# A transposed tile's copy handed from VectorE to ScalarE, three small moves in the same kernel

## The chip, the cores and the metric

One Trainium2 chip, one of its cores. The metric is the device time of one execution in microseconds (us), the median of the timed runs: 208.69 us for the kernel before (three runs, 208.44 to 209.05). The profile is of one execution; its span, from the first to the last instruction, is 206.6 us, so about 2 us of the timed figure lie outside the span.

## What is computed

A block-sparse attention, whose output goes straight into a two-matrix feed-forward stage.

```python
# q, k, v: (4, 8, 768, 64); block 32, window 16
k_sum = k.reshape(B, H, nb, 32, D).max(axis=3)          # 24 block keys
v_sum = v.reshape(B, H, nb, 32, D).mean(axis=3)         # 24 block values
scores_l = scale * q @ k.T, kept where |i - j| < 16
scores_s = scale * q @ k_sum.T + log(32)
a = softmax([scores_l, scores_s])
x = (a @ [v, v_sum])  ->  (B*S = 3072 tokens, H*D = 512)
h = x @ w_in                                             # 512 x 2048
g = h / (1 + exp(-1.702 h))                              # quick gelu
out = g @ w_out                                          # 2048 x 512, fp32
```

## The kernel before

The 3072 tokens are eight half-batches of 384, called units here: u = 0 and 1 belong to batch 0, u = 2 and 3 to batch 1, and so on. For each unit the kernel makes attention scores (ps_s), exponentials (a_sb, on ScalarE), values (ps_av), normalised rows (x, on VectorE), transposes these on TensorE into ps_x, and copies ps_x to SBUF as xT, one copy for each half (g = 0 and 1) of the 512 features. Then `ff_in` (L660) multiplies xT by w_in into PSUM tiles ph, ScalarE takes gelu of each into gT, and `ff_out` (L809) multiplies gT by w_out into po.

Every engine's work stands in program order: the wrapper `_Ordered` (L18) records each instruction so, and nothing overtakes on one engine. So the order in which Python calls are made is the schedule, and it is written out by hand:

- **The head** (L933 to L1028) loads batch 0's keys and queries in fp32 from two issuing engines, SyncE and ScalarE, pair of heads by pair (`load_k`, `load_q`, L83 and L93), then casts (kb, qb), transposes (ps_k, ps_q), copies (kx, qT), takes block maxima (`k_max`, L422, into ksz) and computes unit 0's attention. `exp_soon` (L929) runs a one-element exponential on a tile called gate, so that ScalarE loads the exponential's function table there and not ahead of the first real exponential.
- **Between units 0 and 1** (L1109 to L1122) the output stage of unit 0 has twelve slots. In each, `ff_out` runs four matmuls; then `beside` (L1059) runs what the table `plan0` (L1054) gives for the slot: q's transposes, scores s0 to s3, values v0 and v1, and the transposes with their copies, x0 and x1 (`tx`, L647). After some slots `w_sums` (L825) forms four sums of a quarter of w_out into the tiles ta and tb, on VectorE. Later stages use them for Strassen-Winograd products. After slot 11 `ff_in` of unit 1 starts; its first three ph tiles need x0 for the first six matmuls and x1 for the next six.
- **Unit 1's input stage** also transposes batch 1's keys (ps_t), duplicates batch 1's value rows on VectorE (`v_odd`, L143) and sums them by blocks on TensorE (`vsum`, L316, into ps_vs). The value rows come by six loads of GpSimd's queue (`load_vc`, L137). After these, `halo_dmas` (L347) and `sum_dmas` (L360) bring the edge rows and block sums to their places in vw.
- **The last input stage** (`ff_in_pairs`, L702) handles units 6 and 7 together with seven products, M1 to M7, in place of eight. M6(0) accumulates onto M1(0)'s PSUM tile, and VectorE adds m (M7(0), which ScalarE copied out) to it; M5(0) accumulates onto the same PSUM tile once VectorE has read it. `plain()` (L773) is an ordinary product of four matmuls into a tile of its own.

DMA issues are tied by semaphores: the built program gives the issues of SyncE and ScalarE eight semaphores in turn, and those of GpSimd another eight. A DMA that gets a semaphore for a second time is issued only when the earlier DMA on it has landed. In the head, the fifth issue of ScalarE (keys of pair 3) and its sixth (queries of pair 3) wait in this way; so do GpSimd's issues nearly everywhere.

PSUM tiles of 2 KB (tag mm: po, ph, ps_x, ps_q) rotate through four buffers, those of 4 KB (tag big: ps_s, ps_t, ps_vs, ps_av of unit 1) through two.

Of the kernel before, what the change touches and what calls it, by code (L numbers as in the profile page):

```python
# [35 lines left out]
def kernel(  # L36
# [16 lines left out]
    NP = H // 2  # L53
# [11 lines left out]
    dve = _Ordered(tc, nc.vector)  # L65
    act = _Ordered(tc, nc.scalar)
# [16 lines left out]
    def load_k(p):  # L83
        if p == 0:
            early["k"] = stage.tile([128, NP, 2, 2, JH, D], F32, name="kf", tag="kf")
        t = early["k"][:, p]
        for i in range(2):
            (act if i else sp).dma_start(out=t[:, i].rearrange("p h r d -> p h (r d)"),
                         in_=k[0, 2 * p:2 * p + 2, i * HALF:(i + 1) * HALF]
                         .rearrange("h (p r) d -> p h (r d)", r=JH))  # L90
        raw["k", p] = t
# [159 lines left out]
    def clear0(eng):  # L251

        for p in range(NP):
            clear_kx(eng, p, 0)
        clear_vw(eng, 0)
        eng.memset(ksz, 0.0)
        eng.memset(vs4, 0.0)
        v6 = vs4.rearrange("p (a g) c -> p a g c", g=4)
        for g in range(4):
            eng.memset(v6[g * 32:g * 32 + nb, :, g, D:D + 1], float(block))  # L260
# [386 lines left out]
    def tx(g, m, eng=dve):  # L647
        ps = pmm.tile([128, 2, HALF], F16, name="ps_x", tag="mm")
        for i in range(2):
            for j in range(JH):  # L650
                pe.transpose(out=ps[:, i, j * 128:(j + 1) * 128],
                             in_=x2[g][:, i, j].rearrange("p h d -> p (h d)"), identity=identx)
        copy(eng, xTT[m][g], ps)
# [48 lines left out]
    def ff_in_pairs(u, early):  # L702

        (b11, b21), (b12, b22) = xTT
        xs = castp2.tile([128, 4, 2, HALF], F16, name="xsum", tag="kb")
        t = [xs[:, m] for m in range(4)]
        big = [psb.tile([128, 1024], F32, name="pw_in", tag="big") for _ in range(2)]
        mm = [pmm.tile([128, 512], F32, name="px_in", tag="mm") for _ in range(4)]
        X, V = ([m[:, 0:HALF] for m in mm[n:n + 2]] for n in (0, 2))
        Y = [big[0][:, n:n + HALF] for n in (0, 512)]  # L710
        L = big[1][:, 0:HALF]

        def gelu(w, f, src):
            act.activation(out=gT[w % 2][:, f, :], in_=src, func=ACT.Gelu_apprx_sigmoid)

        def one(w, f, ps):
            for ko in range(KO):
                pe.matmul(out=ps, lhsT=w_in_sb[:, ko, f * 128:(f + 1) * 128], rhs=xT[w % 2][ko],
                          start=(ko == 0), stop=(ko == KO - 1))
            gelu(w, f, ps)  # L720

        def prod(ps, a, b, i, first=False):
            for k in range(2):
                pe.matmul(out=ps, lhsT=a[:, k, i], rhs=b[:, k], start=(first and k == 0),
                          stop=(k == 1), skip_group_check=True)

        ws = [wt["s"][:, n] for n in range(4)]
        hold = {}

        def f0(i):  # L730
            return 2 * (NI - WI + i)

        def M1(i):
            x = X[i % 2]
            prod(x, wt[0, 0], b11, i, True)
            dve.tensor_copy(out=Y[i % 2], in_=x)

        def M7(i):
            v = V[i % 2]
            prod(v, ws[2], t[2], i, True)  # L740
            hold[i] = attp.tile([128, HALF], F32, name="m7", tag="x2")
            copy(act, hold[i], v)

        def M6(i):
            x = X[i % 2]
            prod(x, ws[1], t[1], i)
            dve.tensor_add(V[i % 2], x, hold[i])

        def M2(i):
            y = Y[i % 2]  # L750
            prod(y, wt[0, 1], b21, i)
            gelu(u, f0(i), y)

        def M5(i):
            x = X[i % 2]
            prod(x, ws[0], t[0], i)
            hold[i, 2] = attp.tile([128, HALF], F32, name="c22", tag="a_sb")
            dve.tensor_add(hold[i, 2], x, hold[i])

        def M4(i):  # L760
            v = V[i % 2]
            prod(v, wt[1, 1], t[3], i)
            gelu(u, f0(i) + 1, v)
            gelu(u + 1, f0(i) + 1, hold[i, 2])

        def M3(i):
            x = X[i % 2]
            prod(x, ws[3], b22, i)
            gelu(u + 1, f0(i), x)

        n, rest = 2 * (NI - WI), list(range(2 * (NI - WI)))

        def plain():  # L773
            one(u + 1, rest.pop(0), L)

        for f, ps in zip(range(n), (Y[0], X[1], V[1], L, Y[1], X[1])):
            if f == 2:
                M1(0)
            one(u, f, ps)
        dve.tensor_sub(t[2], b22, b12)  # L780
        dve.tensor_add(t[1], t[2], b11)
        dve.tensor_sub(t[0], b12, b11)
        dve.tensor_sub(t[3], b21, t[1])
        M2(0)
        M7(0)
        plain()
        M6(0)
        for i in range(1, WI):
            M1(i)
            for f in (M7, M5) if i == 1 else (M5, M7):  # L790
                f(i if f is M7 else i - 1)
            M4(i - 1)
            M6(i)
            M3(i - 1)
            M2(i)
            plain()
            if i == 2:
                early(0, NI - WI)
        i = WI - 1
        M5(i)  # L800
        M4(i)
        early(NI - WI, NI)
        plain()
        M3(i)
        assert not rest
# [123 lines left out]
    def exp_soon():  # L929
        act.activation(out=gate[:, 1:2], in_=gate[:, 0:1], func=ACT.Exp)  # L930


    dve.memset(gate, 0.0)  # L933
    for p in range(NP):
        load_k(p)
        load_q(p, 0)
    exp_soon()
    clear0(dve)
    dve.tensor_copy(out=identx, in_=ident)
    dve.memset(vs[:, :, D:VC], float(block))  # L940
# [102 lines left out]
    for p in range(NP):  # L1043
# [8 lines left out]
             6: ["v0", "s2", "s3"], 8: ["x0"], 9: ["v1", "S0", "S1"], 11: ["x1", "S2", "S3"]}  # L1052

    plan0 = {-1: ["q0", "q1"], 0: ["q2"], 1: ["q3"], 2: ["s0", "s1"], 4: ["s2", "s3"],  # L1054
             7: ["v0", "v1"], 9: ["x0"], 11: ["x1"]}

    w51 = vw[1].rearrange("p (j e) h c -> p j e h c", e=2)

    def beside(u, slot):  # L1059
        b, half = u // 2, u % 2  # L1060
        for what in (plan0 if u == 1 else plan1).get(slot, ()):
            i = int(what[1])
            if what[0] == "t":
                tq1(i, dve if i % 2 else act)
            elif what[0] == "q":
                q_turn(i, 1)
                q_copy(i, dve, 1)
            elif what[0] == "s":
                scores(b, half, i)
                if half and i == NP - 1:  # L1070
                    gelu_soon()
            elif what[0] == "S":
                scores(b, 1, i)
                if i == NP - 1:
                    gelu_soon()
            elif what[0] == "v":
                values(b, half, i, u == 1)
            else:
                tx(i, half)

    for u in range(2):
        todo = {}
        if u == 0:
            for p in range(NP):
                todo.setdefault(12 + p // 2, []).append(lambda p=p: cast_q(dve, p, 1))
        else:
            def value_rows():
                vsum(1, range(NJ))
                block_sums()
                halo_dmas(w51, 0)  # L1090
                sum_dmas(w51, 0)
                load_kc(2, range(6, H))
                load_vc(2)
                load_qc(2)

            todo = {0: [lambda: tk(0, 1)], 3: [lambda: tk(1, 1)], 5: [lambda: v_odd(1)],
                    9: [value_rows], 10: [lambda: tk(2, 1)], 13: [lambda: tk(3, 1)]}
            ff_in(u, range(3))
        for nt in range(0 if u else N0, NT):
            if u == 0 or nt > 2:  # L1100
                ff_in(u, (nt,))
            for f in todo.get(nt, ()):
                f()
        exp_soon()
        if u == 0:
            beside(1, -1)
            load_qc(1)
            load_kc(2, range(6))
        order = [(ms, part) for ms in range(JH) for part in range(4)]  # L1109
        if u == 0:  # L1110

            order = [(ms, part) for part in range(4) for ms in range(JH)]
        for i, (ms, part) in enumerate(order):
            ff_out(u, ms, part)
            beside(u + 1, i)
            if u == 0 and i in (4, 7, 10):
                w_sums(i // 3 - 1)
            if u == 1 and i == 2:
                w_sums(3)
            if u == 1 and i == 3:  # L1120
                for g in range(2):
                    xk(g, 2)  # L1122
# [22 lines left out]
    for b in range(1, B):  # L1145
# [3 lines left out]
        u = 2 * b  # L1149
# [95 lines left out]
```

The softmax here doesn't subtract the row's maximum and nothing guards it: scores larger than these inputs give would overflow.

## Time and profile before

| | before |
|---|---|
| time, median of 3 | 208.69 us |
| span of the profiled execution | 206.6 us |
| TensorE busy | 199.2 us, 96% of the span |
| VectorE busy | 145.1 us, 70% |
| ScalarE busy | 123.5 us, 60% |
| GpSimd busy | 91.5 us, 44% |
| chain that ended last | TensorE 90%, VectorE 7%, ScalarE 1%, issue 1% |
| ScalarE copy ps_x to xT, 128x768, mean of 2 | 806 ns |
| VectorE copy ps_x to xT, 128x768, mean of 4 | 553 ns |
| ScalarE function table load, mean of 10 | 1283 ns |
| the four instructions of one `w_sums`, means | 416, 425, 417, 417 ns |

How to read it: nearly the whole chain is TensorE, so a change can bring time only where TensorE's own chain has a hole, and can cost time wherever it opens one. The chain's VectorE part lies mainly in the head and between units 0 and 1. A row of the timeline has the start, the duration (from the first start to the last end, where several are merged), the engine, the operation with its tiles, the count, and, in brackets, how long the engine had been idle and what released it. Matmul durations overlap, so a row's end can lie some 0.15 us past the next row's start.

### The profile page before, as it was taken

To read this page: it belongs to the slowest core of one execution; us is meant where nothing else is said; L and a number is where in the kernel's file an instruction comes from. 1 tells how busy PE (TensorE), PEld (TensorE's weight loads), DVE (VectorE), ACT (ScalarE), POOL (GpSimd) and SP (SyncE) were. 2 spreads that over 40 slices of the span, in tenths; PEclk is the share of its full clock that TensorE was granted. 3 is DMA by queue.
4 is the path that set the end of the run, shared out by engine and by line. 5 is a ranking of instruction groups with operands and counts; after the bars stand their busy time and mean duration, and the time that the engine had idled before them with its cause. 6 is when DMAs were issued, how large, how long until landed. Compare 5 with 4: busy or idle time off the path is not lost.

```text
span 206.6 us, 5570 instructions
## 1 busy us (share of the span) xinstructions
PE 199.2 (96%) x2212; PEld 136.1 (66%) x2212; DVE 145.1 (70%) x421; ACT 123.5 (60%) x235; POOL 91.5 (44%) x162
## 2 busy tenths in 40 slices
PE   7899999998999999999999999999999999999992
PEld 3667565545665666566888865567887855568882
DVE  6677845796966769936757688589885956669431
ACT  0877676634685489677743657677626477881220
POOL 5996889498899951425999100401000000000000
PEclk9999999999999999999999999999999999999999
DMA  6999999999999999999999999993054250000323
GB/s 187 296 166 207 247 246 217 174 171 222 150 155 153 156 128 120 216 133 131 114 129 202 108 274 158 139 165 59 3 129 102 53 179 0 3 2 25 105 76 102
DMA packets 95009, 28.94 MB, mean 140 GB/s; under 512 B 82880, under 2 KB 92000, under 8 KB 94984
## 3 DMA queue, kind: packets, MB, share of 16 engines
q0 software_dynamic: 67920, 14.88, 80.7%
q1 hardware_dynamic: 25432, 12.53, 30.9%
q10 hardware_dynamic: 1632, 1.18, 1.8%
q8 instruction: 17, 0.28, 0.6%
q14 instruction: 8, 0.07, 0.1%
HBM read 27.26 MB, written 6.29 MB: 162 GB/s over the span
## 4 chain that ended last, share of the span: by engine, by line
PE 90%; DVE 7%; ACT 1%; issue 1%; DVEq 0%
PE ph L28 30%; PE px L28 15%; PE pw L28 8%; PE po L28 7%; PE px_in L28 6%; PE ps_av L28 4%; PE ps_s L28 4%; PE py L28 4%; PE pw_in L28 4%; PE ps_w L28 2%; PE ps_t L28 1%; PE ps_k L28 1%; DVE ta L28 1%; PE ps_x L28 1%; DVE x L28 1%; DVE kb L28 1%
## 5 line engine op out<-in xcount | busy, mean ns | idle before, releaser
L28 PE MATMUL ph<-xT,w_in_sb 128*128 128x384 f16 x384 | 65.5, 326 | 1.2 <-DVE xT L28 1.2
L28 PEld LDWEIGHTS <-w_in_sb 128*128 128x128 f16 x462 | 44.3, 98 | 30.3 <-issue 1.7
L28 ACT ACTIVATE gT<-ph 128x384 f16<-128x384 f32 x96 | 45.6, 490 | 21.3 <-PE ph L28 21.0
L28 PEld LDWEIGHTS <-gT 128*128 128x128 f16 x384 | 36.1, 98 | 11.8
L28 ACT ACTIVATE a_sb<-ps_s 128x768 bf16<-128x768 f32 x28 | 21.1, 806 | 8.8 <-PE ps_s L28 8.8
L28 PE MATMUL po<-w_out_sb,gT 128*128 128x512 f16 x96 | 23.4, 380 | 0.0
L28 PEld LDWEIGHTS <-ss 128*128 128x128 f16 x216 | 20.7, 98 | 2.6
L28 ACT ACTIVATE t<-px 128x256 f32<-128x256 f32 x21 | 8.0, 383 | 21.9 <-PE px L28 21.9
L28 DVE TENSOR_TENSOR a_sb<-a_sb,mk 128x768 bf16<-128x768 bf16 x28 | 15.2, 555 | 7.5 <-ACT a_sb L28 6.4
L28 PE MATMUL px<-ta,ss 128*128 128x256 f16 x144 | 18.7, 273 | 0.0
L28 PE MATMUL pw<-tb,gT 128*128 128x256 f16 x144 | 18.7, 273 | 0.0
L28 ACT ACT_TABLE_LOAD x10 | 12.8, 1283 | 6.0 <-DMA kf<-in_k_dram 5.9
L28 DVE TENSOR_TENSOR x<-ps_av,rc 128x384 f16<-128x384 f32 x28 | 15.6, 557 | 1.0
L28 POOL DMA_DIRECT2D vw<-in_v_dram x18 | 15.9, 936 | 0.0
L28 POOL DMA_DIRECT2D vw<-vw x12 | 6.6, 575 | 18.9 <-DVE vw L28 17.2
L28 POOL DMA_DIRECT2D kb<-in_k_dram x16 | 13.2, 856 | 3.5 <-DMA w_out_sb<-in_moe_w_out_dram 3.1
L28 POOL DMA_DIRECT2D qb<-in_q_dram x16 | 13.4, 920 | 2.9 <-DMA vw<-in_v_dram 2.9
L28 DVE TENSOR_TENSOR osb<-pw,t 128x256 f32<-128x256 f32 x18 | 7.5, 421 | 9.0 <-PE pw L28 5.3
L28 DVE TENSOR_TENSOR ss<-gT 128x384 f16<-128x384 f16 (+4 forms) x18 | 7.5, 418 | 5.4 <-ACT gT L28 5.4
L28 PEld LDWEIGHTS <-kx 64*128 64x128 bf16 x400 | 7.2, 95 | 5.8 <-issue 4.0
L28 DVE TENSOR_REDUCE ks<-kx 128x24 bf16<-128x768 bf16 x8 | 7.6, 946 | 3.7 <-DMA kx<-kb 3.7
L28 PE MATMUL ps_s<-qT,kx 64*128 64x64 bf16 (+3 forms) x400 | 9.1, 190 | 0.9 <-DVE kb L28 0.7
(120 smaller groups left out, 311.0 us busy)
## 6 DMA issues: line engine op xcount, KB each, us to landing
out_dram<-osb SPq DMA_DIRECT2D x18, 256.0 KB, 5.0
vw<-in_v_dram POOLq DMA_DIRECT2D x18, 128.0 KB, 6.3
w_in_sb<-in_moe_w_in_dram POOLq DMA_DIRECT2D x4, 512.0 KB, 10.6
w_out_sb<-in_moe_w_out_dram POOLq DMA_DIRECT2D x4, 512.0 KB, 19.8
kb<-in_k_dram POOLq DMA_DIRECT2D x16, 96.0 KB, 5.4
qb<-in_q_dram POOLq DMA_DIRECT2D x16, 96.0 KB, 7.5
out_dram<-osb SPq DMA_DIRECT2D x12, 128.0 KB, 1.7
vw<-vs POOLq DMA_DIRECT2D x6, 148.5 KB, 4.2
```

The lines of the kernel that those rows point to most:

```text
L28: r = f(*a, **kw)
```

## The change

Four edits. (1) The copies of unit 1's x0 and x1 go to ScalarE, and x1 moves from slot 11 to slot 10 of unit 0's output stage, so that its transposes come ahead of the last four po matmuls. (2) The first `w_sums` moves from slot 4 to slot 3, ahead of the scores s2 and s3. The aim of both is that xT stands ready when unit 1's input stage begins. (3) In `ff_in_pairs` M6(0) is put before the first plain product, so that VectorE's addition runs beside that product. (4) In the head the exponential's table is loaded before the last keys and queries are issued, so that ScalarE loads it while it would wait to issue them.

```diff
@@ ff_in_pairs
         M2(0)
         M7(0)
+        M6(0)
         plain()
-        M6(0)
         for i in range(1, WI):
@@ the head
     dve.memset(gate, 0.0)
-    for p in range(NP):
+    for p in range(NP - 1):
         load_k(p)
         load_q(p, 0)
     exp_soon()
+    load_k(NP - 1)
+    load_q(NP - 1, 0)
     clear0(dve)
@@ plan0
-             7: ["v0", "v1"], 9: ["x0"], 11: ["x1"]}
+             7: ["v0", "v1"], 9: ["x0"], 10: ["x1"]}
@@ beside
-                tx(i, half)
+                tx(i, half, act if u == 1 else dve)
@@ the output stage of unit 0
-            if u == 0 and i in (4, 7, 10):
+            if u == 0 and i in (3, 7, 10):
                 w_sums(i // 3 - 1)
```

In the built program this is the whole change of order on each engine, with one thing that the lines do not say: the semaphores of the head's loads are dealt out anew. Before, the fifth issue of SyncE waits for the first keys of SyncE and its sixth for the first queries; ScalarE's fifth waits for its own first keys and its sixth for its own second keys. After, they wait in this order for ScalarE's first keys, SyncE's first keys, ScalarE's second keys, and the first queries. And of the three first ph tiles of unit 1, the third takes the PSUM buffer of x1's transposes, where before it took that of the third po tile.

## The prediction

> **What bounds the kernel now.** I read the page's shares first: TensorE busy 96% of the span, and 90% of the chain that ended last. Only a hole in TensorE's work can bring time. Then the chain in order of time, to find where it leaves TensorE. It does so in the head, between units 0 and 1, and once in the last input stage; from 47.66 us to there it is TensorE without a break. Last the timeline of these stretches. Columns of the chain: start, duration, engine and tile. The head:
>
> ```profile
> 6.40 0.34 PE ps_q L28 x3
> 6.76 0.56 DVE qT L28
> 7.32 1.03 DVE kb L28 x2
> 8.35 0.86 DVE ksz L28
> 9.22 1.04 DVE kb L28 x2
> ```
>
> ScalarE's timeline (start, duration, engine, operation, and in brackets the idle time before it and its releaser) shows there:
>
> ```profile
> 5.85 1.28 ACT L28 ACT_TABLE_LOAD   x1 [5.85 <-DMA kf<-in_k_dram]
> ...
> 7.25 0.79 ACT L28 ACTIVATE kx<-ps_k 128x768 bf16<-128x768 f32 x1
> ```
>
> The load stands behind an issue that waited for a DMA, and kx behind the load; ps_k was done at 6.15. But the chain runs through VectorE's queue, and kx is not on it. Between units 0 and 1:
>
> ```profile
> 43.66 0.41 DVE L28 TENSOR_TENSOR ta<-w_out_sb 128x512 f16<-128x512 f16 x1
> ...
> 44.79 0.41 DVE L28 TENSOR_TENSOR tb<-w_out_sb,ta 128x512 f16<-128x512 f16 x1
> 44.84 0.50 PE L28 MATMUL ps_x<-identx,x 128*128 128x128 f16 x6
> ...
> 45.13 0.55 DVE L28 COPY xT<-ps_x 128x768 f16<-128x768 f16 x1
> 45.59 0.41 DVE L28 TENSOR_TENSOR ta<-w_out_sb 128x512 f16<-128x512 f16 x1
> ...
> 45.73 1.15 PE L28 MATMUL ph<-xT,w_in_sb 128*128 128x384 f16 x6 [0.39 <-DVE xT L28]
> ...
> 47.05 0.55 DVE L28 COPY xT<-ps_x 128x768 f16<-128x768 f16 x1
> 47.66 1.14 PE L28 MATMUL ph<-xT,w_in_sb 128*128 128x384 f16 x6 [0.78 <-DVE xT L28]
> ```
>
> This is the hole to see: x0's transposes were ready at 43.28 and x1's at 45.34, but both copies stand in VectorE's queue behind four sums each. TensorE idles 0.39 and 0.78 us. The last input stage, in the chain:
>
> ```profile
> 170.24 0.34 PE px_in L28 x2
> 170.67 0.58 DVE px_in L28
> 171.29 1.62 PE px_in L28 x8
> ```
>
> M5(0) at 171.29 waits for VectorE's addition to M6(0). M6(0), M1(1) and M7(1) run from 170.24 to 171.22, so the hole is 0.07 us. Last, what could stop a TensorE that comes earlier:
>
> ```profile
> 52.19 1.68 POOL L28 DMA_DIRECT2D qb<-in_q_dram  x2 [0.85 <-DMA vw<-in_v_dram]
> ...
> 53.94 0.52 PE L28 MATMUL ps_vs<-vw,E 128*32 128x128 bf16 x24
> ...
> 60.87 1.36 POOL L28 DMA_DIRECT2D vw<-vs  x2
> ...
> 67.02 0.57 PE L28 MATMUL ps_av<-vw,a_sb 128*64 128x65 bf16 x24
> ```
>
> GpSimd still waits at 52.19 for value loads that ps_vs needs. In the trace's landing records the last of the six lands at 52.66 and the second vw<-vs, which ps_av needs, at 65.69. TensorE passes 1.28 and 1.33 us after these. No engine hurries them: the DMA engines are at 9 tenths or more from slice 2 to 29.
>
> **What the Trainium skill says.** "ScalarE: Activation LUTs", What ACT_TABLE_LOAD costs: about 1283 ns for a load. The trace agrees, 1283 ns mean of 10; the cheap copy is in every set (Table sets: the hidden batching unit), and the trace has ScalarE copying ps_x between gelus without a further load. "PSUM — Partial Sum Buffer", The four PSUM rules: only TensorE, VectorE and ScalarE reach PSUM, so GpSimd can't take the copies. "DMA: Bandwidth & Descriptors", Queues, rings and completion order: each DMA engine goes round its queues packet by packet, so a store or transpose that starts sooner takes turns from GpSimd's loads. The trace before doesn't show such a collision apart.
>
> **Copies and sums (edits 1 and 2).** VectorE loses two copies of 553 ns; ScalarE gains two of 806 ns (row xT<-ps_x, ScalarE, 128x768, mean of 2). ScalarE is free there: 2.55 us idle ahead of its first osb. Rows of a_sb (two in 1.51 us, 806 ns each) show a ScalarE row starting 0.1 us before its predecessor's end, so I take 0.7 us a copy and 0.5 an osb. Its queue becomes: osb of slot 9 at 42.98 as now; x0 at 43.5 to 44.3; osb of slot 10 at 44.2 to 44.8; x1 at 44.7 to 45.5; osb of slot 11 at 45.4 to 46.0. Behind x1 waits only that last osb; behind it gelu, which has its ph no earlier than 46.
>
> TensorE: slot 9 ends at 42.8, x0's transposes 43.12, slot 10 43.98, x1's transposes 44.32, slot 11 45.18. x1 needs its rows from VectorE: now at 43.75, and about 0.3 sooner with the first sums out of the way (at slot 3 they fill VectorE from 37.21, where it idles 1.03 us for an exponential; the masks of s2 and s3 shift from 39.5 to 39.8, needed at 40.6). Either is before 43.98. So ph starts at 45.18. Its third tile reuses x1's PSUM buffer and comes at 45.83, after 45.5. The second six matmuls start at 46.16 for 47.66 now: 1.50 us gained, the two holes of 1.17 and the displayed tails between. The fourth ph tile waits for the last osb, 46.0, and comes at 47.1: no wait.
>
> Then the DMA takes part back. TensorE would be at ps_vs at 53.94 - 1.50 = 52.44; the last value load lands at 52.66, some 0.06 us more to start: 52.72, gain 1.22. VectorE's v_odd, 53.11 now, waits for the same load and gains only 0.4, but its followers have 0.5 us or more until TensorE needs their PSUM buffers. At ps_av, 67.02 - 1.22 = 65.80 against 65.69 + 0.06; here unit 1's store and the key transposes (SyncE, at 64.75 and 65.32 now) start 1.2 us earlier and can hold up those landings. I bound this by 0 and 1 us, and take 0.1: gain 1.1. Later gates have room: batch 2's queries land at 95.38, used at 99.52; its vw at 95.76, used at 107.63; batch 3's queries 139.64 against 143.56. Transposes of x move with TensorE.
>
> **M6(0) (edit 3).** It starts at 169.58 in place of 170.24. Its input xsum is ready at 168.85, m of M7(0) at 170.16, so VectorE adds from 170.2 to 170.8 and M5(0) no longer waits: 0.07 us, at most 0.3 by the weight-load hole beside it. The plain product and its gelu come 0.33 later, into 0.35 us or more of ScalarE's idle time.
>
> **Table load (edit 4).** The load runs from about 2.9 to 4.2, the gate to 4.4. The fifth issue then waits for keys landing at 5.43 (4.03 now), the sixth follows at 5.9 (5.45 now), kx starts at 6.4 in place of 7.25. The first scores come at 7.4, not 8.10, yet VectorE's row 6.76 to 10.25 is unbroken by any wait for ScalarE, so nothing is gained: 0. The price is late loads. With the 5.34 us that the queries issued at 5.45 took, the last keys land at 10.8 for VectorE's cast at 11.49, the queries at 11.3 for GpSimd's at 11.17, whose consumer on TensorE comes at 13.83. Hidden, with 0.7 and over 2 us to spare. Even a gain would meet w_out's first quarter, landing 31.62 for its use at 31.84, so I bound it by 0.2.
>
> Sum: 1.1 + 0.07 + 0 = 1.17, which gives 208.69 - 1.17 = 207.5 us.
>
> **Rivals.** *The halo gate moves* (chance 0.20): stores and transposes, earlier by 1.2, delay vw<-vs by some 0.7, and ps_av waits. Against it: they begin to move about when the last halo lands. Gain 1.22 - 0.75 + 0.07 = 0.5: 208.2. *No gate bites* (0.13): value loads land 0.3 earlier because fewer descriptors compete, and the head gives 0.2. Gain 1.50 + 0.07 + 0.2: 206.9. Against it: the loads depend on GpSimd's issues, which the change leaves alone. *The head loses* (0.14): the last keys, issued 1.4 later, land among GpSimd's value loads not at 10.8 but at 13, VectorE stalls 1.5 and the SyncE reshuffle adds to it; with w_out and the vw gates also late, of 1.17 nothing is left: 208.69 - 1.17 + 1.5 = 209.0. For it: from issue to landing kf takes 4.1 to 5.9 us. Against: loads issued in the same stretch took 5.2 to 5.3.
>
> **Numbers.** The main course has 0.53. Range: 206.7 takes in the second rival, 208.6 the first with its 1 us bound; the head's loss is left out. Faster by over 0.3% means below 208.06: the main course, the second rival, and a little of the first, 0.70; within 0.3% most of the first and a mild head loss, 0.17; slower 0.13.
>
> **What would show it.** Right: no VectorE releaser in front of ph after slot 11, the second six matmuls near 46.2, ps_vs near 52.7 with a short idle released by a value load, ps_av near 65.9; M5(0) without a wait; in the head kx at 6.4 with VectorE's rows where they are. Wrong: a wait of VectorE for kf near 11.5, ph waiting for ScalarE, ps_av after 66.5, or a head whose ps_vt comes earlier than 15.4.

## The result and the profile after

| | before | after |
|---|---|---|
| time, median | 208.87 us (208.44 to 209.27) | 207.27 us (207.03 to 207.58) |
| ratio after / before, 95% interval | | 0.9925 (0.9899 to 0.995) |
| span of the profiled execution | 206.6 us | 205.3 us |
| TensorE busy | 199.2 us | 197.7 us |
| VectorE / ScalarE busy | 145.1 / 123.5 us | 143.6 / 124.9 us |

The change is worth 1.57 us by the ratio (208.87 × 0.0075; 1.04 to 2.11 by its interval); the prediction said 1.17. The profiled execution of the kernel before took 208.35 us, under all four of its timed ones; that of the kernel after took 207.03, the shortest of its four. So 1.7 us of a time lie outside the span in both, not about 2, and the two profiles differ by 1.32 us where the medians differ by 1.60. The page's chain that ended last, by engine, now reads (ACTq is ScalarE issuing a DMA):

```profile
PE 93%; DMA 3%; ACTq 1%; DVE 0%; ACT 0%; issue 0%
```

VectorE's 7% are gone from the chain, and something new has come in: 3% of a DMA. Follow the three places that the prediction showed. Between units 0 and 1, the timeline after (start, duration, engine, operation, idle time before and its releaser):

```profile
43.55 0.60 ACT L28 ACTIVATE osb<-po 128x512 f32<-128x512 f32 x1 [2.55 <-PE po L28]
44.05 0.81 ACT L28 ACTIVATE xT<-ps_x 128x768 f16<-128x768 f16 x1
...
44.55 0.50 PE L28 MATMUL ps_x<-identx,x 128*128 128x128 f16 x6
...
44.75 0.60 ACT L28 ACTIVATE osb<-po 128x512 f32<-128x512 f32 x1
...
45.24 0.81 ACT L28 ACTIVATE xT<-ps_x 128x768 f16<-128x768 f16 x1
...
45.75 2.11 PE L28 MATMUL ph<-xT,w_in_sb 128*128 128x384 f16 x12
```

The two groups of six ph are one row of twelve, with no wait. From the first po of unit 0 to the twelfth ph of unit 1 TensorE took 16.79 us before (31.68 to 48.47) and takes 15.28 after (32.26 to 47.54): 1.51 us less. But the stretch starts 0.58 us later than before. The head shows one reason, in the chain after (start, duration, piece):

```profile
1.33 5.66 DMA kf<-in_k_dram
...
7.01 0.37 ACTq L28
...
7.42 0.49 ACTq L28
...
7.96 0.82 ACT kx L28
...
8.82 0.45 PE ps_s L28 x16
```

and in ScalarE's timeline:

```profile
2.92 1.28 ACT L28 ACT_TABLE_LOAD   x1 [2.92 <-issue]
...
7.01 0.37 ACTq L28 DMA_DIRECT2D kf<-in_k_dram  x1
7.42 0.49 ACTq L28 DMA_DIRECT2D qf<-in_q_dram  x1
7.96 0.81 ACT L28 ACTIVATE kx<-ps_k 128x768 bf16<-128x768 f32 x1 [3.54 <-DMA kf<-in_k_dram]
```

The table load went where the edit meant it to go. But ScalarE's second keys landed at 6.99 us where they had landed at 5.43 in the profile before. The trace has sixteen updates for a load, one for each part: fifteen had come by 5.43, the last came 1.56 us later. Until then the fifth issue waits, and kx stands behind it. Last, the last input stage: VectorE's addition to M6(0), and the row of TensorE's chain at that place.

```profile
169.14 0.57 DVE L28 TENSOR_TENSOR px_in<-px_in,m 128x384 f32<-128x384 f32 x1 [0.44 <-ACT m L28]
```

```profile
169.50 2.11 PE px_in L28 x12
```

VectorE adds while the plain product runs, and the pause before M5(0) is gone. The two gates that the prediction feared (a gate is here a DMA's landing for which TensorE may have to wait), in the timeline after:

```profile
53.01 0.52 PE L28 MATMUL ps_vs<-vw,E 128*32 128x128 bf16 x24
...
60.78 1.27 POOL L28 DMA_DIRECT2D vw<-vs  x2
...
66.08 0.57 PE L28 MATMUL ps_av<-vw,a_sb 128*64 128x65 bf16 x24
```

By the landing records the last value load came at 52.50 and the second vw<-vs at 65.57, both ahead of TensorE. The sum of this profile: −1.51 (hole) + 0.58 (first po later) − 0.23 (last input stage) − 0.12 (a pause between 120 and 131 us which the profile before has and nearly every later one lacks, with or without the edits) = −1.28; the spans differ by 1.3.

### The profile page after: what moved, and what is told of

The parts are those of the page before. It is cut to its first block, busy times and chain, and to the rows that moved or that the text cites. A ratio compares the mean times of both kernels' runs of the same rounds, so it can differ in the third digit from the quotient of the medians.

```text
span 205.3 us, 5570 instructions
## 1 busy us (share of the span) xinstructions
PE 197.7 (96%) x2212; PEld 135.4 (66%) x2212; DVE 143.6 (70%) x419; ACT 124.9 (61%) x237; POOL 92.0 (45%) x162
## 4 chain that ended last, share of the span: by engine, by line
PE 93%; DMA 3%; ACTq 1%; DVE 0%; ACT 0%; issue 0%
PE ph L28 31%; PE px L28 16%; PE po L28 10%; PE pw L28 8%; PE px_in L28 6%; PE ps_av L28 5%; PE ps_s L28 4%; PE py L28 4%; PE pw_in L28 4%; DMA kf<-in_k_dram 3%; PE ps_x L28 1%; PE ps_t L28 1%; PE ps_k L28 1%; PE ps_q L28 1%; PE ps_vs L28 1%; ACTq L28 1%
```

## The experiments

One table carries most of what follows: how much later TensorE reached a point than in the profile before, in us, from the trace of one execution each. The columns are the head's end (first ps_vt, 15.37 before), the first po of unit 0 (31.68), the twelfth ph of unit 1 (48.47), the last ps_vs (54.24), the first ph of unit 2 (74.59, behind ps_av), the first product of the last input stage (164.46) and the end (202.91).

| | head | first po | 12th ph | ps_vs | unit 2 | last stage | end |
|---|---|---|---|---|---|---|---|
| after | 0.47 | 0.58 | −0.93 | −0.93 | −0.94 | −1.06 | −1.29 |
| after2 | 0.87 | 0.91 | −0.60 | −0.60 | −0.07 | −0.20 | −0.44 |
| x_only | 0.19 | 0.07 | −1.43 | −1.44 | −0.98 | −1.11 | −1.11 |
| no_table | 0.55 | 0.51 | −0.99 | −0.99 | −0.95 | −1.08 | −1.31 |
| m6_only | 0.59 | 0.77 | 0.77 | 0.77 | 0.77 | 0.64 | 0.41 |
| table_only | −0.04 | 0.11 | 0.10 | 0.10 | 0.10 | −0.03 | −0.02 |
| act_only | 0.27 | 0.87 | −0.41 | −0.41 | −0.41 | −0.54 | −0.54 |
| slot_only | 0.23 | 1.09 | 0.15 | 0.15 | 0.14 | 0.01 | 0.01 |
| act_slot | −0.19 | 0.21 | −1.30 | −1.02 | −0.33 | −0.46 | −0.45 |
| x_halo | −0.15 | 0.92 | −0.60 | −0.60 | −0.61 | −0.73 | −0.73 |
| sp_last2 | −0.36 | 0.00 | −1.51 | −1.19 | −0.99 | −0.96 | −1.20 |
| gates | 0.99 | 0.87 | −0.64 | −0.64 | −0.64 | −0.77 | −1.00 |

Read it by differences between columns. First po to twelfth ph is the hole; to ps_vs and to unit 2 are the two gates; last stage to end is edit 3. Everything up to the first po varies from execution to execution.

### Each part alone

**x_only**, edits 1 and 2 alone:

```diff
-             7: ["v0", "v1"], 9: ["x0"], 11: ["x1"]}
+             7: ["v0", "v1"], 9: ["x0"], 10: ["x1"]}
-                 tx(i, half)
+                 tx(i, half, act if u == 1 else dve)
-             if u == 0 and i in (4, 7, 10):
+             if u == 0 and i in (3, 7, 10):
```

> Edits 1 and 2 alone (ScalarE's copies, x1 one slot earlier, first sums one slot earlier). Theory, the hole between units 0 and 1 is what the change filled and no later gate takes it back: 1.5 us less than before, ph without a VectorE wait, the twelve ph matmuls of unit 1 unbroken. Rival, the gain is limited by batch 1's value loads, which land near 52.6: TensorE waits at ps_vs and 1.2 us are left. In the trace, an idle of TensorE ahead of ps_vs, released by a DMA, tells them apart.

Measured: 207.22 us, ratio 0.9917 (0.989 to 0.9944). The hole gives 1.50 (0.07 to −1.43). TensorE, coming at 52.51, was not stopped at ps_vs, though the last value load landed at 52.55. At ps_av it was; TensorE's timeline of x_only:

```profile
65.58 0.22 PE L28 MATMUL ps_av<-vw,a_sb 128*64 128x65 bf16 x1
66.06 0.54 PE L28 MATMUL ps_av<-vw,a_sb 128*64 128x65 bf16 x23 [0.27 <-DMA vw<-vs]
```

One matmul runs on rows that are there, the other 23 wait for the second vw<-vs, which landed at 65.93. Of 1.44 us 0.98 is left behind it. So the second gate is real, and it takes 0.46.

**m6_only**, edit 3 alone (the two lines of `ff_in_pairs` in the change's diff).

> Edit 3 alone. Theory, what the profile after shows (the work following M6(0) 1.06 us earlier ahead of it, 1.29 after it): 0.23 us less than before. Rival, the prediction's count of the chain's hole: 0.07 us. Both lie near what timing can tell; the distance in the trace from the first pw_in matmul of the last input stage to its end tells them apart: 0.23 or 0.07 us shorter.

Measured: 208.46 us, ratio 0.9978 (0.9964 to 0.9992), 0.46 us by the ratio (0.17 to 0.75 by its interval, which takes in 0.23 and not 0.07). In the profile the last stage gives 0.23 (0.64 to 0.41). Every profile with edit 3 gives 0.23 or 0.24 there, and every one without it 0 or 0.01.

**table_only**, edit 4 alone (the head's lines of the change's diff).

> Edit 4 alone. Theory, the load's new place costs time whenever it runs: ScalarE's kx stands behind the issue of the last keys, and the head is 0.5 to 0.6 us longer as in the profile after, so 0.5 us more than before. Rival, that profile had one late DMA engine (the second keys of ScalarE landed at 6.99, fifteen of sixteen parts at 5.43): where they land by 5.5, kx starts at 6.4 and nothing changes, within 0.1 us of before. Second rival: before is as exposed to the same late landing and loses more by it, so on the mean this is 0.2 us less.

Measured: 208.56 us, ratio 0.9985 (0.9968 to 1.0002). That is not told from no change. Here the second keys landed at 5.55, kx started at 6.52, almost where the prediction put it, and the head ended 0.04 us from where it had ended: an earlier kx alone gains nothing where the keys land as soon as this.

**no_table**, edits 1, 2 and 3, that is the change without edit 4.

> Edits 1, 2 and 3, without 4. If the table load's place costs 0.5 us, this takes 206.7 to 206.9 (the value loads at 52.6 taking back up to 0.2). If it costs nothing on the mean, the same as with all four, 207.3. If it helps, 207.5.

Measured: 207.66 us, ratio 0.9923 (0.9904 to 0.9943). The change with edit 4 has 0.9925 (0.9899 to 0.995). Edit 4 adds nothing that these times can tell. The trace of no_table shows a place for it all the same. The second keys landed at 6.07, the table load (ACT at 6.50) stands behind the issue that waits for them, kx behind the load, and the head ends 0.55 late. In its chain:

```profile
1.32 4.75 DMA kf<-in_k_dram
...
6.50 1.28 ACT L28
...
8.00 0.71 ACT kx L28
```

### Engine or queue order

Edit 1 changes the engine of the copies and the slot of x1. These three kernels take it apart.

**act_only**: only `tx(i, half, act if u == 1 else dve)`; x1 stays in slot 11.

> The engine alone: unit 1's two copies go to ScalarE, x1 stays in slot 11, the sums where they were. If the copies waited because of VectorE's queue, the first six ph start without a wait (0.4 us sooner than before) and the second six wait only for x1's own copy behind the osb of slot 11: near 46.4 in the clock of the kernel before, for 47.66 (1.2 us gained). Rival (the slot was what mattered): the second six come after 47, and less than 0.6 us is gained.

**slot_only**: only `10: ["x1"]`; VectorE copies.

> The slot alone: x1 in slot 10, its copy still on VectorE but now ahead of the sums of slot 10 instead of behind them. If standing behind the sums was the cause, the second six ph come near 46.7 to 46.9 in the clock of the kernel before, for 47.66, so 0.8 to 1.0 us is gained with VectorE still copying, and the first six stay behind VectorE's earlier sums. Rival (VectorE is too slow for these copies wherever they stand): VectorE releases both, and less than 0.4 us is gained.

**act_slot**: both, and the first sums left behind slot 4, so edit 1 without edit 2.

> Edit 1 without edit 2: copies on ScalarE, x1 in slot 10, the first sums left after slot 4. Theory (the first sums only have to end before x1's rows are wanted, and do so either way): from the first po to the twelfth ph of unit 1 it takes 15.3 us as with both edits (15.28 in edits 1 and 2 alone, 16.79 in the kernel before). Rival (edit 2 is what brings x1's rows forward in time): 15.6 us or more, with VectorE's x in front of x1's transposes.

Measured, from the first po to the twelfth ph: before 16.79 us; act_only 15.51, a gain of 1.28; slot_only 15.85, a gain of 0.94; act_slot 15.28, a gain of 1.51, the same as with edit 2. VectorE and TensorE in slot_only's timeline:

```profile
45.87 0.42 DVE L28 TENSOR_TENSOR tb<-w_out_sb,ta 128x512 f16<-128x512 f16 x1
46.21 1.01 DVE L28 COPY xT<-ps_x 128x768 f16<-128x768 f16 x2
```

```profile
46.82 2.12 PE L28 MATMUL ph<-xT,w_in_sb 128*128 128x384 f16 x12 [0.40 <-DVE xT L28]
```

Both copies run back to back, ahead of the third sums, and ph runs as one row of twelve: VectorE is fast enough. What held x1 was where its copy stood. The first 0.40 us remain, since x0 still stands behind the second sums. Either remedy gets most of the hole, together they get all of it, and edit 2 adds nothing to the two. The single times (207.78, 208.33 and 207.91 us) say little, because the first po came 0.87, 1.09 and 0.21 us late in them. Part of that lateness has a name; slot_only's TensorE:

```profile
32.77 1.04 PE L28 MATMUL po<-w_out_sb,gT 128*128 128x512 f16 x4 [0.69 <-DMA w_out_sb<-in_moe_w_out_dram]
```

The first quarter of w_out landed at 32.73 us here, at 31.62 before. In 7 of the 13 profiles (before and the table's twelve) the first po starts 0.06 to 0.91 us later than TensorE's own work would let it, and 0.04 to 0.05 us after that landing. The changed kernel is one: its ps_q at 31.86 would let po start at 32.20 (the 0.34 us between the two in the profile before), w_out landed at 32.22, po started at 32.26. So, if w_out doesn't land sooner with them, punctual keys alone would have gained it 0 here.

### The head and the gates

**after2**, the changed kernel once more.

> The changed kernel once more, to part what comes from the change in its head from what varies from execution to execution. Theory (a late part of the second keys is chance, and edit 4 makes the head indifferent to it up to a landing at 6.5 us): the second keys land at 5.4 to 6.3 us, kx starts at 6.4 to 6.6 and the head is as in the kernel before (ps_vt at 15.3 to 15.6); the first po then comes 0.05 us behind the landing of w_out's first quarter or at 31.7, whichever is later. Rival (the new order of the loads delays the keys): they land at 6.9 again and ps_vt comes at 15.8.

Measured: 207.91 us in this execution. The second keys landed at 5.13 and kx started at 6.35, as the prediction had it. The head was later still, by 0.87, for another reason. Pair 1's keys come in two halves: ScalarE's second keys are one, and SyncE issues the other at 1.83 us. This other half landed at 8.33 where it had landed at 7.02 before, and VectorE's casts waited for it. VectorE's timeline of after2, then TensorE's:

```profile
8.36 1.05 DVE L28 CAST kb<-kf 128x384 bf16<-128x384 f32 x2 [1.61 <-DMA kf<-in_k_dram]
```

```profile
9.21 0.83 PE L28 MATMUL ps_k<-ident,kb 128*128 128x128 bf16 x6 [1.54 <-DVE kb L28]
```

From these casts VectorE works on without a break, as it does from 7.24 in the kernel before, and its copy of pair 1's transposed queries (qT) comes at 11.04 for 10.17: that is the 0.87. Neither theory had this. The queries of pair 1 landed late too (8.77), but their cast on ScalarE (qb) ended at 9.31, and TensorE came to transpose them only at 9.83, behind the six ps_k. And at ps_av, in TensorE's timeline of after2:

```profile
66.46 0.19 PE L28 MATMUL ps_av<-vw,a_sb 128*64 128x65 bf16 x1
66.98 0.54 PE L28 MATMUL ps_av<-vw,a_sb 128*64 128x65 bf16 x23 [0.32 <-DMA vw<-vs]
```

The second vw<-vs landed at 66.84, 1.27 later than in the other execution of the same kernel. With the late first po and this wait, 0.44 us of the gain is left in this profile.

**sp_last** and **sp_last2**, the same kernel: the change, with all of the last pair's loads issued by SyncE, so that ScalarE has four loads and waits to issue none.

```diff
-             (act if i else sp).dma_start(
+             (act if i and p < NP - 1 else sp).dma_start(
-         (act if p % 2 else sp).dma_start(
+         (act if p % 2 and p < NP - 1 else sp).dma_start(
```

> All four edits, and the last pair's keys and queries issued by SyncE alone, so that ScalarE has four loads to issue and never waits to issue one. Both theories expect ScalarE's kx at 6.3 to 6.6 us whenever the second keys of ScalarE land, so a head no later than in the kernel before (first po at 31.7 or sooner, against 32.26 in the changed kernel's profile). Theory (the second vw<-vs gates ps_av): the head's gain ends there, TensorE waits for a landing at about 65.9, and the time is that of the changed kernel, 207.1 to 207.3 us. Rival (the gate doesn't hold a TensorE that comes with an undisturbed head): the 0.5 us carry to the end, 206.7 us or less. Second rival: the last pair's loads, all behind each other on one issuing engine, come too late for VectorE's cast of the last keys and the head loses 0.5 us or more.

> The kernel with the last pair's loads on SyncE once more, for a profile, since the first one was of an execution of 511 us, in which every matmul took twice its time. Expected: kx at 6.3 to 6.6 us whatever the landing of the second keys, since ScalarE waits for no issue. If the last keys and queries, queued behind SyncE's own four loads, land late, VectorE's cast of the last keys waits (after 11.6) and ps_vt comes after 15.6; if not, ps_vt comes at 15.2 to 15.4 and the wide spread of its times has another source.

Measured: 207.63 us, ratio 0.9952 (0.9932 to 0.9973), with single times from 206.45 to 209.48: not better than the change, with a spread that is not explained here. The first profile is of an execution of 511 us, whose matmuls ph took 685 ns for 326, and is left aside. In the second, kx starts at 5.56, sooner than expected (ps_k was done), the head ends first of all (−0.36), and w_out, landing at 31.50, doesn't hold the first po. With the hole filled TensorE is then 1.51 early, and both gates bite. TensorE's timeline of sp_last2:

```profile
52.44 0.84 PE L28 MATMUL ps_vs<-vw,E 128*32 128x128 bf16 x24
...
65.84 0.77 PE L28 MATMUL ps_av<-vw,a_sb 128*64 128x65 bf16 x24
```

Rows that take 0.52 and 0.57 us elsewhere take 0.84 and 0.77: the waits lie inside them. 0.32 and 0.20 us are lost, for landings at 53.00 and 65.93.

**x_halo**: edits 1 and 2, and two of batch 2's key loads moved behind the halo and sum transfers in GpSimd's queue.

```diff
-             load_kc(2, range(6))
+             load_kc(2, range(4))
-                 load_kc(2, range(6, H))
+                 load_kc(2, range(4, H))
```

> Edits 1 and 2 alone, and two of batch 2's key loads moved in GpSimd's queue from ahead of the halo and sum transfers to behind them, so that vw<-vs is issued some 1.6 us sooner. Theory: edits 1 and 2 alone lose 0.46 us of their 1.50 at ps_av because vw<-vs lands at 65.9; here it lands near 64.3, TensorE doesn't wait at ps_av, and what the hole gave goes through to the end: 1.4 us below the kernel before in the profile, 206.8 to 207.0 us in time. Rival: another transfer takes the gate's place (the key loads come too late for the transposes of batch 2, or the vw<-vs land no sooner since the DMA engines are full): 207.2 us as with edits 1 and 2 alone, or more.

Measured: 207.30 us, ratio 0.9931 (0.9904 to 0.9958), not told from x_only. Two things spoiled it as a test. w_out landed at 32.55, so TensorE reached ps_av only at 66.42; and the second vw<-vs was issued at 60.96 and landed at 65.01, 0.9 sooner than in x_only and not 1.6.

**gates**: the change, with the first quarter of w_out as two halves, and all eight of those key loads behind the halo and sum transfers.

```diff
-         pool.dma_start(out=w_out_sb[:, c * 4:(c + 1) * 4, :],
-                        in_=wo[:, c * 4:(c + 1) * 4, :])
+         for a in ((0, 2) if c == 0 else (0,)):
+             e = a + (2 if c == 0 else 4)
+             pool.dma_start(out=w_out_sb[:, c * 4 + a:c * 4 + e, :],
+                            in_=wo[:, c * 4 + a:c * 4 + e, :])
-             load_kc(2, range(6))
-                 load_kc(2, range(6, H))
+                 load_kc(2)
```

> The changed kernel with both DMA gates opened: the first quarter of w_out loaded as two halves (so that the first po matmul waits only for a half that should land 1 us or more before 32.2 us), and all eight of batch 2's key loads moved in GpSimd's queue behind the halo and sum transfers, so that vw<-vs can be issued near 57 us and not at 60.7. Theory (two landings at the brink, w_out's first quarter and the second vw<-vs, hold TensorE up after the hole is filled): no wait for w_out at 32, vw<-vs lands at 63 or sooner, no wait at ps_av, and the time is 206.7 us or less when the head is undisturbed, 0.5 us below the changed kernel. Rival (the DMA engines are full, so what one transfer gains another loses): a later transfer, the key rows of batch 2 or the value loads behind them, becomes the wait, and the time is 207.2 us or more.

Measured: 206.94 us (206.79 to 207.78), ratio 0.9917 (0.9891 to 0.9942). That is the lowest median of all kernels here, but its interval lies on that of the change. The profile shows the gates open. GpSimd's timeline, and TensorE's:

```profile
55.03 2.15 POOL L28 DMA_DIRECT2D vw<-vw  x4 [0.71 <-DVE vw L28]
57.21 1.36 POOL L28 DMA_DIRECT2D vw<-vs  x2
58.67 6.98 POOL L28 DMA_DIRECT2D kq<-in_k_dram  x8
```

```profile
66.38 0.57 PE L28 MATMUL ps_av<-vw,a_sb 128*64 128x65 bf16 x24
```

The halves of w_out landed at 30.50 and 32.30 for a first po at 32.55 and cost nothing; the second vw<-vs landed at 62.74, 3.6 us ahead of its use; no later transfer became a wait. The head was 0.99 late in that execution. Again SyncE's half of pair 1's keys came late, at 8.30, with VectorE's casts behind it; in the chain:

```profile
1.84 6.47 DMA kf<-in_k_dram
...
8.33 1.20 DVE kb L28 x2
```

So TensorE came too late to show what the open gates are worth: that waits for an execution with a punctual head, and is open.

## Why the prediction was right, and where its steps were not

**Copies and sums: right.** Predicted 1.50; measured 1.50 to 1.52 in all eight profiles with edit 1 whole. ScalarE's queue runs in the order and at the intervals of the working (osb, x0, osb, x1, osb; 0.5 us behind an osb, 0.7 behind a copy). The row of twelve starts at 45.75, so its seventh matmul comes at 46.73, and without the 0.58 us by which the stretch began late that is 46.15, for a predicted 46.16. That edit 2 isn't needed was in the step (x1's rows come before 43.98 with it or without it), and act_slot shows it.

**ps_vs: the step was mis-sized.** The prediction put the wait ahead of the first matmul and charged 0.28 us. The code of `vsum` takes the six loads one after another, four matmuls each, so only the last four need the last load. x_only arrives 0.04 before that landing and loses nothing; act_slot and sp_last2, with landings at 53.17 and 53.00, lose 0.28 and 0.32. In the changed kernel it took 0.

**ps_av: right in kind, its share not a constant.** The prediction charged 0.1 and bounded it by 1. It took 0 in one profile of the changed kernel, 0.53 in the other, 0.46 in x_only, 0.69 in act_slot. In act_slot the first of the two vw<-vs, landing at 66.07, holds the first matmul too. What decides is two times that both vary, that of TensorE and that of the second landing: 65.57 to 66.84 where GpSimd's order was left alone. The rival "the halo gate moves", forecast at 208.2, comes near the time of after2 (207.91), but its cause is not shown. It had slower transfers; in after2 the second vw<-vs was issued 0.90 later than in the other execution of the kernel (62.34 for 61.44) and took 4.50 us to land for 4.13. In the six profiles with the hole filled and GpSimd's order left alone it took 4.13 to 4.66, in the five others of that order 3.56 to 4.18, so stores and transposes that come earlier may have a part in it; that stays open. One reading was wrong beside this: the page's DMA row stands at 9 from slice 2 to 27, not to 29. The gates lie in slices 11 and 13, so nothing hangs on it.

**The table load: right for the head that was read, but one landing was taken for a fixed time.** "The fifth issue then waits for keys landing at 5.43" took one landing of one profile as given. In the two profiles of the change the second keys landed at 6.99 and 5.13, in all thirteen at 5.13 to 6.99, and kx started at 7.96 and 6.35, for a predicted 6.4. The value, 0, holds as far as times tell: table_only against before, and no_table beside the change, show nothing. What edit 4 does is seen in the traces. In the eight profiles without it kx starts 1.82 to 1.83 us after the second keys land; in after, table_only and gates it starts 0.96 to 0.97 after. In no_table and m6_only, which lack edit 4 and where the keys landed at 6.07 and 6.27, the chain runs through that stretch and the head is 0.55 and 0.59 late. So "kx is not on it" was true of the one head that the prediction read; in heads such as these two edit 4 should gain. That is inferred, and no run shows it. Whether edit 4 itself delays SyncE's half of pair 1's keys is open: in its five profiles SyncE issues its sixth load at 4.40 to 4.69 us where it had been 5.16 to 5.59, and that half landed at 7.21 (after), 8.33 (after2), 8.30 (gates), 6.95 (table_only) and 6.71 (sp_last2), against 6.52 to 7.61 in the eight without it.

**What the prediction saw but did not charge.** w_out's first quarter was named as a limit for a gain of the head, with 0.2 us to spare. It is a gate that holds the first po in more than half of the profiles, by up to 0.91 us. It stands ahead of the hole, so it moves the hole and doesn't eat it.

**M6(0): mis-sized.** Predicted 0.07, measured 0.23, within the 0.3 that the step named as its bound. The step took the end that the chain gives to M7(1), 171.22, for the moment at which TensorE ran dry. Such ends are modelled; the starts tell more. TensorE's timeline before, and then after, has the same four matmuls, two of M7(1) and two of M5(0), as one row:

```profile
170.72 1.05 PE L28 MATMUL px_in<-xsum,wsum 128*128 128x384 f16 x4
```

```profile
169.66 0.81 PE L28 MATMUL px_in<-xsum,wsum 128*128 128x384 f16 x4
```

The pause inside the first row is the difference, 0.24 us. It is shown as no idle time, since rows that lie close are merged. Its size could have been read from the trace before, where four matmuls of this kind without a pause take 0.81 (px_in and pw_in, x4).

**The sum.** Predicted 1.50 − 0.28 − 0.12 + 0.07 = 1.17. In the changed kernel's profile the hole and edit 3 bring 1.74, and 0.58 of it is lost ahead of the hole, to a first po that came late; the gates took nothing there. So in this profile the 0.40 charged for gates stood in for a lateness that was not charged: that the sum comes out near is luck there. Over several executions the two are in part tied together. A TensorE that comes late can find the gates open (after, 0.93 early: no loss), one that comes early is stopped (x_only, 1.43 early: 0.98 left; sp_last2, 1.51 early: 0.99 left), so about 1 us is left of the hole in these three against the profiled head of the kernel before. It is no rule: in after2 and act_slot, where the second vw<-vs landed at 66.84 and 66.58, 0.07 and 0.33 are left. Why the timed gain, 1.57, is above 1.17 is not shown. One clue is that the profile of the kernel before is of an execution 0.52 us below the median of its timed ones, and that of the kernel after of one only 0.24 below: the two profiles differ by 0.28 less than the medians. Late heads in the timed executions of the kernel before, against which the gates cost nothing, would explain it, but no profile of one was taken. The interval holds 1.17 as well.

## What to carry to other kernels

A copy that TensorE waits for is priced by what stands ahead of it in its engine's queue: moving it, with its transposes, one slot up and past four sums on the same engine gave 0.94 of 1.51 us here, and moving it to an engine that was idle just then gave 1.28. Before charging a DMA gate, find the first instruction that needs the last landing, not the first of the group, and treat the landing as a range: one profile gives one draw of it. Where landings stand at the brink on both sides of an edit, compare stretches between two points of one trace (16.79 us before, 15.27 to 15.29 in every kernel with edit 1 whole), since ends and single times mix the edit with the luck of the head.

## What the runs showed of the hardware beyond what was expected

- The same 192 KB load, issued at the same place in the head, landed anywhere from 5.13 to 6.99 us; in the latest case 15 of its 16 parts were there 1.56 us before the last. SyncE's half of the same pair's keys, issued at 1.83 or 1.84, landed from 6.52 to 8.33, and w_out's first quarter, loaded whole, from 31.50 to 32.73.
- A DMA issue that waits for its semaphore stops the compute behind it: kx, which needs nothing of the keys that it stood behind, started at 7.96 us in one execution and at 6.35 in the other of the same kernel.
- Six transfers moved ahead of six key loads in GpSimd's queue landed some 3 to 4 us sooner (the second vw<-vs at 62.74, for 65.57 to 66.84), and the trace shows no wait of TensorE for a transfer behind them.
